# q transposed on VectorE in 32x32 blocks, kv and u on eight TensorE tiles, one PSUM ring and a new hand-written order

## The chip, the cores and the metric

The kernel runs on one core of a Trainium2 chip. The metric is device time in microseconds (us) of one execution; the time before is the median of three runs. The engines are named as the profile names them: PE is TensorE (its matmuls; PEld its weight loads), DVE is VectorE, ACT is ScalarE, POOL is GpSimd, SP is SyncE, which here only issues DMAs.

## What is computed

A linear attention with a normalised output, followed by a channel mix. B = 8 batches, H = 8 heads, S = 576 positions, 64 dims per head; all inputs and the output are fp32. C = 512, F = 1024.

```python
def _attn_ref(q, k, v, g_norm):
    kv = np.einsum('bhsd,bhse->bhde', k, v)
    out = np.einsum('bhsd,bhde->bhse', q, kv)
    rms = np.sqrt(np.mean(out * out, axis=-1, keepdims=True) + 1e-06)
    return (out / rms * g_norm).astype(np.float32)

def _moe_ref(x, mu_k, mu_r, w_k, w_v, w_r):
    x_prev = np.concatenate([np.zeros((B, 1, D)), x[:, :-1, :]], axis=1)
    xk = mu_k * x + (1.0 - mu_k) * x_prev
    xr = mu_r * x + (1.0 - mu_r) * x_prev
    k = np.maximum(xk @ w_k, 0.0)
    v = k * k @ w_v
    r = 1.0 / (1.0 + np.exp(-(xr @ w_r)))
    return (r * v).astype(np.float32)
```

The attention's heads are laid side by side as the 512 channels of x. Matmuls run in bf16 with fp32 sums in PSUM.

## The kernel before, in words

**Layout.** All activations of the second half stand with channels on the partitions: a batch's x is four chunks of 128 channels (two heads each, e = 0 and 1), handled as two halves z = 0 and 1 of two chunks each (y). k, v and q are loaded by POOL DMAs that cast to bf16, with position s = 9p + j on 64 partitions p per head and nine column blocks j (NJ = 9, NP = 64). The kernel keeps that permuted order of positions (j, then p) up to the stores.

**Attention of one batch** (`attention`, line 362). `kv` (L286): for each head nine matmuls of 64x64 sum k.T v; four heads' tiles are in use at a time. `q` (L294): 36 transposes of 64x64 per half through the identity matrix into PSUM, then a copy `qc` to SBUF on ACT or DVE. `u` (L301): kv times q, per half z and half of the positions i, four matmuls of 64x64 tiles over 288 columns. `uc` copies u to bf16, `sq` squares it (ACT from PSUM, or DVE from the copy), `ss` sums the squares over a head's 64 dims by a matmul (with a block of 1/64 for batches 0 and 1, L432 and L464; with 32 columns per chunk, L409, and a spread by eight SP DMAs per batch, `sp`, L455, from batch 2 on). `rs` (L306) is the reciprocal root on ACT, `mul` (L423) the product of u and rs into an x buffer `xT`.

**The blend** (`blends`, line 311). In the permuted order the position before is 64 columns earlier, and the first block's predecessors are the last block's, shifted by one: `wr` copies those 63 columns in front of `xT`. Then `d` = cur - prev (L318), `mk` and `mr` = d times mu (a scalar per partition, L178 on ACT or L180 on DVE), `xk` and `xr` = m + prev (L331), written to a ring of four batches. In batch 0 this is done in parts `a`, `b` and a wrapped part `w`.

**The channel mix** (`mix`, line 496) works on nine groups g of 512 positions. `k` (L542; L518 for group 0): eight blocks of four matmuls, `relu` on ACT, `ksq` on DVE; `r` (L564): four blocks of four, `sig` on ACT; `v` (L584): four rows of 128 positions in two parts of four matmuls, `out` on DVE = v times sig, `st` the stores on SP (row blocks of up to 64 positions, so mostly two DMAs each). g_norm is put into w_k and w_r in place (`g.wk`, `g.wr`), by a column `cols` that a small matmul `tr9` makes from mu_k, mu_r and g.

**The order.** Each piece of work has a name such as `u3.01` or `k4.6`, registered by `add` with what it depends on. The text `ORDER` lists the names; `emit` (line 84) issues them in that order, so it is each engine's own order, with `@A` (ACT) or `@D` (DVE) where a choice is open. `ld.*` are the load DMAs on POOL. `z:512` is a matmul of zeros on PE that nothing needs. PSUM is four tiles of two banks, two of them tagged `mm` (for k, r, v) and two `at` (for the attention and `ss`); SBUF buffers are rings too (k, v, q three each, qT, uT four or three).

Of the kernel before, what the change touches and what calls it, by code (L numbers as in the profile page):

```python
# [7 lines left out]
FP32 = mybir.dt.float32  # L8
BF16 = mybir.dt.bfloat16
# [6 lines left out]
ld.q0.0 seta small setb ld.k0.0 ld.v0.0 ld.q0.1 ld.v0.1 ld.k0.1 ident ld.wk0 id9 ld.q1.0 z:512 z:512 z:512 z:512  # L16
z:512 z:512 z:512 z:512 z:512 z:512 z:512 q0.01 ld.wk1 tr9 qc0.01@A cols z:512 q0.00 qc0.00@A ld.v1.1 z:512 z:512
z:512 z:512 z:512 z:512 z:512 z:512 kv0.0 ld.v1.0 kc0.0@A z:512 u0.01 u0.00 uc0.01@D uc0.00@A ld.k1.1 sq0.01@D
sq0.00@D z:512 z:512 z:512 z:512 z:512 ss0.01 ss0.00 rs0.01 ld.k1.0 rs0.00 mul0.01 z:512 z:512 q0.11 qc0.11@D ld.wr
mul0.00 z:512 kv0.1 q0.10 d0.0a kc0.1@A qc0.10@D mk0.0a@A z:512 u0.11 uc0.11@D u0.10 wr0.0@A sq0.10@A d0.0w sq0.11@D  # L20
uc0.10@A g.wk00@D ld.q1.1 z:512 z:512 z:512 z:512 ss0.10 xk0.0a d0.0b ss0.11 rs0.10 k0.000 ld.wv0 rs0.11 mul0.10
q1.0 g.wk01@A d0.1a mk0.1a@D mk0.0b@A xk0.1a mr0.0a@D table k0.001 g.wk10@D ld.wv1 g.wk11@D k0.010 mul0.11 relu0.00
d0.1b ld.q2.01 xk0.0b k0.011 mk0.0w@D mk0.1b@D k0.100 wr0.1@D relu0.01 xk0.1b ld.v2.01 d0.1w ksq0.00 k0.101 mr0.0b@A
mr0.1a@D k0.110 ld.k2.01 relu0.10 xr0.0b ksq0.01 mr0.1b@A xk0.0w ksq0.10 ld.v3.01 kv1 qc1.0@D kc1@A xr0.1b mr0.0w@A
xr0.0a u1.01 u1.00 uc1.01@A k0.111 uc1.00@A g.wr1@D ld.k3.01 g.wr0@D relu0.11 sq1.01@D r0.2 sq1.00@D ld.q3.01
mr0.1w@D mk0.1w@D ss1.0 xr0.0w ss1.1 ksq0.11 rs1.0 r0.3 xr0.1a rs1.1 q1.1 r0.0 qc1.1@D ld.k6.01 xr0.1w mul1.0 u1.11
sig0.1 u1.10 r0.1 uc1.11@D sq1.10@A v0.1.0 sq1.11@D sig0.0 xk0.1w ld.q4.01 uc1.10@D ss1.2 v0.1.1 wr1.0@D d1.0 ss1.3
v0.0.0 mk1.0@D rs1.2 xk1.0 v0.0.1 ld.v4.01 rs1.3 q2.0 mul1.1 q2.1 qc2.0@A v0.3.0 wr1.1@D d1.1 v0.3.1 out0.0 mk1.1@A
v0.2.0 st0.1 qc2.1@A xk1.1 v0.2.1 mr1.1@D k1.2 out0.1 k1.3 mr1.0@D kv2 relu1.1 k1.0 kc2@D ld.k4.01 xr1.0 ld.q5.01
u2.10 u2.01 uc2.10@D k1.1 uc2.01@A sq2.01@A sq2.10@D k1.6 relu1.0 u2.11 u2.00 uc2.11@A k1.7 uc2.00@D sq2.11@D k1.4  # L30
sq2.00@A xr1.1 relu1.3 k1.5 ksq1.3 ss2 kv3 ksq1.1 rs2 q3.0 ld.k5.01 sp2.0 r1.0 kc3@A relu1.2 qc3.0@D r1.1 ksq1.0
u3.01 q3.1 uc3.01@D sp2.1 r1.2 ld.q6.01 sq3.01@D ld.v5.01 r1.3 sig1.0 qc3.1@D ld.v6.01 ksq1.2 u3.00 u3.10 v1.0.0
uc3.00@D uc3.10@A st0.0 sq3.10@A sq3.00@D v1.0.1 sig1.1 mul2.0 u3.11 q4.1 wr2.0@D d2.0 v1.1.0 mk2.0@A v1.1.1 mul2.1
v1.3.0 qc4.1@A out1.0 v1.2.0 wr2.1@A xk2.0 uc3.11@A st1.0 v1.2.1 sq3.11@A d2.1 v1.3.1 st0.3 mk2.1@D xk2.1 ss3 kv4
out1.1 q4.0 k2.2 ld.q7.01 qc4.0@D rs3 ld.v7.01 k2.3 kc4@D sp3.0 mr2.1@D u4.11 u4.00 uc4.11@D k2.4 uc4.00@A relu2.1
sq4.11@D k2.5 sq4.00@D sp3.1 mr2.0@D u4.01 relu2.2 u4.10 uc4.01@D k2.0 sq4.10@A sq4.01@D k2.1 ksq2.1 uc4.10@A st1.1
xr2.0 ss4 relu2.0 q5.1 xr2.1 k2.6 ksq2.0 k2.7 mul3.0 qc5.1@D r2.0 relu2.3 r2.1 wr3.0@A ksq2.3 rs4 r2.2 ksq2.2 sp4.0
d3.0 r2.3 sig2.0 mk3.0@D q6.1 mul3.1 kv5 sig2.1 q5.0 qc6.1@D st1.3 v2.3.0 kc5@A qc5.0@D v2.1.0 st0.2 wr3.1@D d3.1
u5.11 u5.01 sp4.1 uc5.11@A v2.2.0 mk3.1@D uc5.01@A xk3.1 v2.3.1 mr3.1@D v2.2.1 sq5.01@D st1.2 sq5.11@D v2.0.0 xk3.0
out2.1 u5.10 kv6 uc5.10@A q6.0 ld.k7.01 mul4.0 v2.0.1 st2.2 qc6.0@A mr3.0@D v2.1.1 kc6@A sq5.10@D st2.3 xr3.1 k3.2  # L40
out2.0 u6.10 u5.00 k3.3 uc5.00@A mul4.1 st2.0 k3.4 xr3.0 relu3.1 wr4.1@D k3.5 d4.1 uc6.10@A r3.0 mr4.1@D relu3.2
sq5.00@D r3.1 sq6.10@D wr4.0@D ksq3.1 u6.01 sig3.0 ss5 uc6.01@D k3.0 d4.0 k3.1 sq6.01@D mk4.1@D rs5 kv7 mr4.0@D
relu3.0 q7.0 sp5.1 xr4.0 u6.00 k3.6 kc7@A ksq3.2 qc7.0@A k3.7 mk4.0@D ksq3.0 r3.2 relu3.3 sp5.0 uc6.00@D r3.3
sq6.00@D xk4.0 u6.11 q7.1 uc6.11@D v3.1.0 st2.1 ksq3.3 v3.0.0 sig3.1 mul5.1 v3.1.1 qc7.1@A sq6.11@D xk4.1 ss6 xr4.1
v3.0.1 r4.0 out3.0 r4.1 rs6 st3.0 u7.10 u7.11 sq7.10@A v3.2.0 uc7.11@A st3.1 uc7.10@D v3.3.0 sq7.11@D wr5.1@D sp6.0
u7.00 mul5.0 u7.01 v3.2.1 sig4.0 d5.1 v3.3.1 uc7.00@A wr5.0@A k4.6 sq7.00@A out3.1 sq7.01@A k4.7 uc7.01@A mk5.1@D
st3.2 ss7 d5.0 relu4.3 k4.2 sp6.1 mk5.0@D mr5.1@A k4.3 xk5.0 k4.4 ksq4.3 relu4.1 xr5.1 k4.5 xk5.1 k4.0 relu4.2
mul6.0 k4.1 mr5.0@D wr6.0@A d6.0 r4.2 relu4.0 r4.3 ksq4.0 k5.2 ksq4.1 sig4.1 mul6.1 k5.3 ksq4.2 v4.1.0 mr6.0@D rs7
xr5.0 v4.1.1 relu5.1 sp7.1 v4.0.0 wr6.1@A ksq5.1 v4.0.1 r5.0 out4.0 sp7.0 r5.1 mk6.0@D v4.3.0 d6.1 v4.2.0 mr6.1@D
st4.1 sig5.0 mk6.1@D v4.3.1 xk6.0 v4.2.1 k5.4 out4.1 k5.5 xr6.0 st4.3 k5.0 relu5.2 xk6.1 k5.1 mul7.1 st4.0 wr7.1@A  # L50
k5.6 relu5.0 d7.1 st3.3 k5.7 ksq5.0 k6.6 ksq5.2 relu5.3 xr6.1 k6.7 mk7.1@D k6.0 relu6.3 mr7.1@D k6.1 ksq6.3 r6.2
# [48 lines left out]
def kernel(  # L100
# [20 lines left out]
    NJ = 9  # L121
    NP = S // NJ
    HS = S // 2
    NZ = NHP // 2
# [6 lines left out]
    CB = 2  # L131

# [8 lines left out]
        "q": (3, (128, NHP, NJ * HD), BF16),  # L141
        "kv": (2, (128, 2, NZ * HD), BF16),
        "qT": (4, (128, 2, S), BF16),
# [10 lines left out]
        "mm": (2, (128, 2, 512), FP32),  # L154
        "at": (2, (128, 2, 512), FP32),
# [4 lines left out]
    def get(buf, dtype=None):  # L160
        if buf.t is None:
            n, shape, dt = BUFS[buf.tag]
            pool = psum if buf.tag in ("mm", "at") else sb
            buf.t = pool.tile(list(shape), dt, tag=buf.tag, name=buf.tag, bufs=n)
        return buf.t

    def as_bf16(ps):
        return get(ps)[:, :, :].bitcast(BF16)
# [21 lines left out]
    ident = const.tile([128, 128], BF16, name="ident")  # L190
# [12 lines left out]
    xTs = [const.tile([128, 2, NP + S], BF16, name=f"xT{i}") for i in range(NX)]  # L203

    src = {"k": k, "v": v, "q": q}
    kvq = {(n, b): Buf(n) for n in src for b in range(B)}

    def setup_a(_):
        nc.vector.memset(zero, 0.0)  # L209
        nc.vector.memset(ident, 0.0)  # L210

    def setup_b(_):
        nc.vector.memset(eps, 1e-6)
        nc.vector.memset(ones, 0.0)
# [12 lines left out]
    def small_loads(_):
# [134 lines left out]
    def attention(b):  # L362
# [28 lines left out]
        else:  # L391
# [261 lines left out]
```

## Time and profile before

| what | value |
|---|---|
| median of three runs | 209.66 us (209.08 to 210.3) |
| span of the profiled execution | 206.6 us |
| granted TensorE clock, mean | 1.000 |
| PE: transposes of q (L294) | 576 matmuls, 8.0 us busy |
| PE: kv (L286) and u (L301) | 576 and 128 matmuls, 6.4 and 7.9 us busy |
| PE: k, r, v (L518, L542, L564, L584) | 7.6 + 59.2 + 34.1 + 66.6 us busy |
| ACT relu, sig, table loads | 36.8, 18.3, 15.4 + 1.3 us busy |
| loads: q, k, v and weights | 35 DMAs on POOL, 16.78 MB as written |
| HBM read, written | 33.56 MB, 9.44 MB |

The profile is of one execution, and its span, 206.6 us, runs from its first instruction to its last; the median of the runs is 3.06 us longer, and that difference is taken as what lies around the span. Matmuls are pipelined, so a duration of one, such as 379 ns, is longer than the distance to the next, 0.216 us for 512 columns (16 of them in 3.45 us on the chain of waits). Lines with PE in them are known by L294 (transposes of q), L286 (kv), L301 (u), L409, L432 and L464 (sums of squares), L482 (zeros), and L518, L542, L564, L584 (k, r, v).

### The profile page before, as it was taken

The numbers are of one execution on the slowest core, as the hardware profiler recorded it, in microseconds if no ns is written. First come the engines' busy times: TensorE is split into PE (matmuls) and PEld (weight loads), VectorE is DVE, ScalarE is ACT, GpSimd is POOL, SyncE is SP. The second block draws the span as 40 slices with busy tenths as digits, with TensorE's granted clock in tenths as the row PEclk, the third lists the DMA queues.
The fourth block names the chain that finished last, engine by engine and source line by source line (L and its number), as shares of the span: only waits on it lengthen the run. The fifth ranks groups of instructions, "written<-read, shape, count | busy, mean of one in ns | idle before, by whom it ended". The sixth has DMA issues, their size and how long they took to land.

```text
span 206.6 us, 5133 instructions
## 1 busy us (share of the span) xinstructions
PE 193.2 (94%) x2172; PEld 95.7 (46%) x2172; DVE 137.8 (67%) x273; ACT 118.6 (57%) x151; POOL 26.4 (13%) x40
## 2 busy tenths in 40 slices
PE   7797979999799799799999999999999999999992
PEld 2344844544344444354443585444444444444441
DVE  1059988886585999698997798788733623421332
ACT  2279789867577395636896987716725032531310
POOL 7752532202140400000000000000000000000000
PEclk9999999999999999999999999999999999999999
DMA  4999999999999999999433650346004242604155
GB/s 75 162 207 205 206 208 205 208 216 221 210 238 236 231 252 242 223 264 268 116 91 77 149 122 0 71 94 156 0 0 102 62 93 61 143 0 102 24 133 153
DMA packets 25211, 30.10 MB, mean 146 GB/s; under 512 B 2524, under 2 KB 20708, under 8 KB 25188
## 3 DMA queue, kind: packets, MB, share of 16 engines
q0 software_dynamic: 15408, 16.78, 48.3%
q1 hardware_dynamic: 9380, 12.46, 24.0%
q10 hardware_dynamic: 400, 0.52, 0.7%
q8 instruction: 17, 0.28, 0.5%
q14 instruction: 6, 0.05, 0.1%
HBM read 33.56 MB, written 9.44 MB: 208 GB/s over the span
## 4 chain that ended last, share of the span: by engine, by line
PE 68%; DMA 20%; SPq 3%; ACT 2%; POOL 2%; issue 2%; DVE 1%; ACTq 0%; DVEq 0%; POOLq 0%
PE mm L584 26%; PE mm L542 24%; PE mm L564 12%; DMA w_r<-in_moe_w_r_dram 7%; DMA rs<-rsc 5%; DMA k<-in_k_dram 4%; DMA out_dram<-out 3%; SPq L455 2%; PE at L584 2%; PE at L301 2%; PE at L286 1%; PE at L294 1%; SPq L493 1%; POOL q L251 1%; ACT rsc L306 1%
## 5 line engine op out<-in xcount | busy, mean ns | idle before, releaser
L584 PE MATMUL mm<-w_v,sqk 128*128 128x512 bf16 x272 | 62.6, 379 | 0.0
L542 PE MATMUL mm<-xk,w_k 128*128 128x512 bf16 (+1 forms) x288 | 59.2, 356 | 0.0
L503 ACT ACTIVATE relu<-mm 128x1024 bf16<-128x1024 f32 x36 | 36.8, 1022 | 25.8 <-PE mm L542 23.4
L584 PEld LDWEIGHTS <-sqk 128*128 128x128 bf16 x296 | 28.2, 98 | 32.2 <-issue 1.4
L542 PEld LDWEIGHTS <-w_k 128*128 128x128 bf16 x288 | 27.2, 98 | 26.9 <-issue 1.6
L564 PE MATMUL mm<-w_r,xr 128*128 128x512 bf16 x144 | 34.1, 379 | 0.7 <-DVE w_r L180 0.7
L552 DVE TENSOR_TENSOR sqk<-relu 128x1024 bf16<-128x1024 bf16 x32 | 21.6, 687 | 16.4 <-ACT relu L503 16.4
L597 DVE TENSOR_TENSOR out<-mm,sig 128x1024 f32<-128x1024 f32 x16 | 19.6, 1222 | 18.6 <-PE mm L584 18.6
L574 ACT ACTIVATE sig<-mm 128x1024 bf16<-128x1024 f32 x18 | 18.3, 1024 | 22.5 <-PE mm L564 22.5
L564 PEld LDWEIGHTS <-xr 128*128 128x128 bf16 x144 | 13.7, 98 | 16.6 <-issue 1.0
L180 DVE TENSOR_SCALAR md<-d,cols 128x576 bf16<-128x576 bf16 (+2 forms) x62 | 18.2, 344 | 0.3
L172 ACT CAST uT<-at 128x576 bf16<-128x576 f32 (+1 forms) x18 | 11.4, 645 | 11.4 <-PE at L301 11.3
L423 DVE TENSOR_TENSOR xT<-uT,rs 128x1152 bf16<-128x1152 bf16 (+2 forms) x18 | 12.4, 686 | 4.8 <-DMA rs<-rsc 3.0
L188 ACT ACT_TABLE_LOAD x12 | 15.4, 1283 | 0.2
L174 DVE CAST uT<-at 128x576 bf16<-128x576 f32 (+1 forms) x14 | 10.4, 742 | 7.0 <-PE at L301 5.5
L318 DVE TENSOR_TENSOR d<-xT 128x1152 bf16<-128x1152 bf16 (+2 forms) x20 | 12.7, 634 | 0.8 <-ACT xT L172 0.5
L331 DVE TENSOR_TENSOR xk<-md,xT 128x1152 bf16<-128x1152 bf16 (+2 forms) x20 | 12.7, 633 | 0.6 <-ACT md L178 0.4
L331 DVE TENSOR_TENSOR xr<-md,xT 128x1152 bf16<-128x1152 bf16 (+2 forms) x20 | 12.5, 631 | 0.0
L482 PE MATMUL mm<-zero 128*128 128x512 bf16 x34 | 10.9, 452 | 1.2 <-DVE zero L209 1.2
L172 ACT COPY qT<-at 128x1152 bf16<-128x1152 bf16 (+2 forms) x8 | 8.0, 995 | 6.0 <-PE at L294 6.0
L178 ACT ACTIVATE md<-d,cols 128x256 bf16<-128x256 bf16 (+2 forms) x18 | 9.9, 600 | 1.8 <-DVE d L318 1.8
L174 DVE COPY qT<-at 128x1152 bf16<-128x1152 bf16 (+2 forms) x10 | 6.9, 693 | 4.7 <-ACT kv L172 4.2
(54 smaller groups left out, 139.3 us busy)
## 6 DMA issues: line engine op xcount, KB each, us to landing
out_dram<-out SPq DMA_DIRECT2D x67, 128.0 KB, 2.5
q<-in_q_dram POOLq DMA_DIRECT2D x6, 576.0 KB, 23.0
v<-in_v_dram POOLq DMA_DIRECT2D x6, 576.0 KB, 25.7
k<-in_k_dram POOLq DMA_DIRECT2D x6, 576.0 KB, 22.5
rs<-rsc SPq DMA_DIRECT2D x48, 72.0 KB, 5.0
q<-in_q_dram POOLq DMA_DIRECT2D x4, 288.0 KB, 9.7
k<-in_k_dram POOLq DMA_DIRECT2D x4, 288.0 KB, 11.4
v<-in_v_dram POOLq DMA_DIRECT2D x4, 288.0 KB, 11.0
```

What stands on the lines that cost most here:

```text
L172: nc.scalar.copy(out=dst, in_=src)
L174: nc.vector.tensor_copy(out=dst, in_=src)
L180: nc.vector.tensor_scalar(out=dst, in0=src, scalar1=col, scalar2=None, op0=ALU.mult)
L188: nc.scalar.preload_act_table_set(name)
L331: nc.vector.tensor_tensor(out=dst[:, 2 * z:2 * z + 2, r0:r0 + w], in0=md.t[:, :, cs], in1=xT[:, :, prev], op=ALU.add)
L503: nc.scalar.activation(out=get(rt), in_=ps.t, func=AF.Relu)
L542: nc.tensor.matmul(get(ps)[:, fc % 2, a0:a1], w_k_sb[:, cc, 128 * fc:128 * fc + 128], xk[:, cc, x0:x0 + a1 - a0], start=(cc == 0), stop=(c ...
L552: nc.vector.tensor_mul(out=get(sqk)[:, 2 * f2:2 * f2 + 2, :], in0=rt.t, in1=rt.t)
L564: nc.tensor.matmul(get(ps)[:, ci % 2, :], xr[:, cc, n0:n0 + 128], w_r_sb[:, cc, :], start=(cc == 0), stop=(cc == NHP - 1))
L574: nc.scalar.activation(out=get(sg), in_=ps.t, func=AF.Sigmoid)
L584: nc.tensor.matmul(get(ps)[:, bank, cs], sqk.t[:, fc, 128 * ci:128 * ci + 128], w_v_sb[:, fc, cs], start=(fc == 0), stop=(fc == NFC - 1))
L597: dv = add(f"out{g}.{c2}", "D", lambda _, ps=ps, sg=sg, ot=ot: nc.vector.tensor_mul(out=get(ot), in0=ps.t, in1=sg.t), deps=ms + [sg_done], ...
```

## The change

- **q.** The load takes q as it lies in memory: partition p holds 36 consecutive positions of one head (16 partitions per head), 2304 bf16 values. Read as fp32, a value is a pair of dims. DVE transposes blocks of 32x32 of these pairs (`tq`, two instructions per batch, 18 blocks each), writing with a step of 36 fp32 elements, so that positions come out in natural order. Chunk m's pairs of dims then stand on partitions 32m to 32m + 31, and head e's positions in columns S*e on, the two dims of a pair (r) next to each other. The PE transposes, their copies `qc` and the 128x128 identity go; a 9x9 one stays for `tr9`.
- **kv and u.** kv takes every second column of k for each r and writes 32 partitions per chunk: 144 matmuls of 64x32 tiles per batch, eight tiles in turn. u sums r = 0 and 1: 16 matmuls of 32x64 tiles per word, each over 288 columns, reading every second element of qT. A word `u3.01.0` covers both halves z (batch 0 has one word per z), and so two PSUM tiles.
- **g** is the factor of the u copy `uc` (ACT or DVE); the weights are used as loaded. `sq` reads u, without g, from PSUM, and only on ACT.
- **Natural order.** `wr` and batch 0's `w` parts go; prev is the column just before cur. `xk` = cur + (mu - 1) * d, so `cols` gets mu - 1. A store is one DMA of 128 rows.
- **PSUM** is one ring of four tiles, `ps`, for everything; the zero matmuls hold one of them until group 0.
- **Loads**: w_k in halves of rows instead of columns; the order after batch 0 is wk0, wk1, wr, batch 1, wv0, wv1, batch 2.
- **Order**: all words in a new order. Choices of engine: `uc` 14 on ACT and 18 on DVE (were 18 and 14), `mk` and `mr` 15 and 21 (9 and 31), `kc` 5 and 4 (7 and 2); `sq` 32 on ACT (10 on ACT, 22 on DVE). Table loads of ACT between rs and sig by the order: 9 (were 11).

```diff
@@ ORDER, its head @@
-ld.q0.0 seta small setb ld.k0.0 ld.v0.0 ld.q0.1 ld.v0.1 ld.k0.1 ident ld.wk0 id9 ld.q1.0 z:512 z:512 z:512 z:512
...
+seta ld.q0.0 ld.k0.0 ld.v0.0 tq0.0.1 setb tq0.0.0 ident ld.q0.1 ld.v0.1 ld.k0.1 small
+zz z:512 z:512 z:512 z:512 z:512 z:512 z:512 z:512 z:512 z:512 tr9 z:512 z:512 z:512 z:512 z:512 z:512 z:512 z:512 z:512 z:512 z:512 z:512 z:512 z:512 z:512 z:512 z:512 z:512 z:512 z:512 z:512 z:512 z:512 z:512 kv0.0 cols ld.wk0 ld.wk1 kc0.0@D z:512 u0.0.0 uc0.00@D ld.wr u0.0.1 uc0.01@D
+tq0.1.0 ld.v1.0 tq0.1.1 ld.q1.01 ld.k1.1 sq0.00 z:512 ss0.00 sq0.01 ld.k1.0 ld.v1.1 ss0.01 z:512 z:512 z:512 kv0.1
+ld.wv0 rs0.01 mul0.01 rs0.00 kc0.1@A z:512 z:512 z:512 u0.1.0 u0.1.1 ld.wv1 sq0.10 z:512 ss0.10 mul0.00 d0.01
+mk0.01@D d0.00 mr0.01@D uc0.10@A mk0.00@D rs0.10 mul0.10 ld.v2.01 sq0.11 z:512 z:512 z:512 z:512 z:512 ss0.11 xk0.01 k0.100
+ld.k2.01 d0.10 mk0.10@D xk0.00 uc0.11@A rs0.11 mul0.11 k0.000 k0.010 k0.110 d0.11 xk0.10
+mk0.11@A xk0.11 xr0.01 mr0.11@D k0.011 mr0.10@A xr0.10 mr0.00@A xr0.00 k0.101 relu0.01 xr0.11
+k0.111 relu0.10 relu0.11 ksq0.10 r0.2 r0.3 sig0.1 r0.0 ld.q2.01 k0.001 relu0.00 r0.1
+tq1.01.0 ksq0.11 ksq0.01 kv1.01 tq1.01.1 kc1.01@D u1.01.0 ksq0.00 sig0.0 table sq1.10 u1.01.1
+sq1.11 sq1.00 sq1.01 uc1.10@D v0.2.0 uc1.11@D ss1.2 v0.3.0 uc1.01@D uc1.00@D rs1.2 ss1.3
+rs1.3 mul1.1 ss1.1 rs1.1 ss1.0 rs1.0 d1.1 mul1.0 mk1.1@A d1.0 mr1.1@D v0.3.1
+xk1.1 mk1.0@A v0.1.0 v0.1.1 v0.0.0 v0.2.1 mr1.0@A v0.0.1 xk1.0 out0.0 kv2.01 kc2.01@A
+k1.0 k1.1 relu1.0 out0.1 st0.3 k1.2 tq2.01.1 k1.3 relu1.1 tq2.01.0 u2.01.0 sq2.10
...
@@ buffers @@
-        "q": (3, (128, NHP, NJ * HD), BF16),
-        "kv": (2, (128, 2, NZ * HD), BF16),
-        "qT": (4, (128, 2, S), BF16),
+        "q": (3, (128, QJ * HD), BF16),
+        "kv": (2, (128, 2, 2 * HD), BF16),
+        "qT": (2, (128, 2 * S, 2), BF16),
...
-        "mm": (2, (128, 2, 512), FP32),
-        "at": (2, (128, 2, 512), FP32),
+        "ps": (4, (128, 2, 512), FP32),
@@ kv, u @@
+    def kv_tiles(ps, kin, vin, ms):
+        for r in range(2):
+            for j in range(NJ):
+                for m in ms:
+                    for e in range(2):
+                        rows_ = slice(64 * e, 64 * e + 64)
+                        nc.tensor.matmul(ps[32 * m:32 * m + 32, e, HD * r:HD * r + HD],
+                                         kin[rows_, m, HD * j + r:HD * j + HD:2], vin[rows_, m, HD * j:HD * j + HD],
+                                         start=(j == 0), stop=(j == NJ - 1))
+
+    def u_tiles(pss, kv, qT, zs, c0, c1):
+        for r in range(2):
+            for z in zs:
+                for y in range(2):
+                    for e in range(2):
+                        m = 2 * z + y
+                        rows_ = slice(32 * m, 32 * m + 32)
+                        nc.tensor.matmul(pss[z][64 * e:64 * e + 64, y, 0:c1 - c0], kv[rows_, e, HD * r:HD * r + HD],
+                                         qT[rows_, S * e + c0:S * e + c1, r], start=(r == 0), stop=(r == 1))
@@ blends @@
-        cur, prev = slice(NP + x0, NP + x0 + w), slice(x0, x0 + w)
+        cur, prev = slice(X0 + x0, X0 + x0 + w), slice(X0 - 1 + x0, X0 - 1 + x0 + w)
...
-in0=md.t[:, :, cs], in1=xT[:, :, prev],
+in0=md.t[:, :, cs], in1=xT[:, :, cur],
@@ attention @@
+                def tq(_, i=i, part=part):
+                    src = qin.t.bitcast(FP32).rearrange("q (j i) -> q j i", i=32)
+                    dst = get(qT).rearrange("q t r -> q (t r)").bitcast(FP32).rearrange("q (p j) -> q j p", j=QJ)
+                    js = slice(QJ // 2 * i, QJ // 2 * i + QJ // 2)
+                    nc.vector.transpose(out=dst[part, js, :], in_=src[part, js, :])
...
+                uc = add("uc" + name, "DA", lambda eng, ps=ps, uT=uT, cs=cs, w=w: scale(
+                    eng, get(uT)[:, :, cs], ps.t[:, :, 0:w], cols[:, 8:9]), deps=[pu[(z, i)], p_cols], bufs=[ps, uT])
+                sq_ = add("sq" + name, "A", lambda _, ps=ps, sq=sq, cs=cs, w=w: nc.scalar.activation(
+                    out=get(sq)[:, :, cs], in_=ps.t[:, :, 0:w], func=AF.Square), deps=[pu[(z, i)]], bufs=[ps, sq])
@@ store @@
+    def store(g, ci, ot, cs=slice(None), eng=None):
+        row = G * g + 128 * ci
+        (eng or nc.sync).dma_start(out=out_rows[row:row + 128, cs], in_=ot)
```

QP = 16, QJ = 36 and X0 = 2 are new constants.

## The prediction

> **What bounds it now.** I read the page first, then the chain of waits in order of time, then the timeline of PE, ACT, DVE and POOL in the first 45 us and of PE between 45 and 104 us, last the groups split by shape.
>
> ```profile
> span 206.6 us, 5133 instructions
> PE 193.2 (94%) x2172; PEld 95.7 (46%) x2172; DVE 137.8 (67%) x273; ACT 118.6 (57%) x151; POOL 26.4 (13%) x40
> ...
> PE   7797979999799799799999999999999999999992
> ...
> DVE  1059988886585999698997798788733623421332
> ...
> DMA  4999999999999999999433650346004242604155
> ```
> PE is full from about 30 us to 203 us; the 16 DMA engines are full until about 95 us; VectorE (DVE) is near full in several slices between 60 and 115 us, but seldom the last to arrive. The chain in order of time (start, length, what):
>
> ```profile
> 29.04 0.89 DVE w_r L180 x2
> ...
> 29.97 1.02 PE mm L564 x4
> ...
> 43.43 1.73 PE mm L542 x8
> 45.16 0.74 PE at L286 x72
> 45.89 0.97 PE mm L542 x4
> 46.86 0.37 PE at L301 x8
> ...
> 91.00 0.25 PE at L301 x4
> ...
> 201.05 1.76 PE at L584 x16
> ```
> So before 30 us the loads decide (w_r lands at 29.0), and after it the work of PE itself. PE's own idle after 30 us is small, and the timeline names it:
>
> ```profile
> 54.39 0.48 PE L294 MATMUL at<-ident,q 64*64 64x64 bf16 x36 [1.20 <-DMA q<-in_q_dram]
> ...
> 68.42 0.83 PE L286 MATMUL at<-v,k 64*64 64x64 bf16 x72 [0.93 <-DMA k<-in_k_dram]
> ...
> 71.81 0.44 PE L301 MATMUL at<-qT,kv 64*64 64x288 bf16 x8 [0.42 <-DVE kv L174]
> ...
> 84.16 0.77 PE L286 MATMUL at<-v,k 64*64 64x64 bf16 x72 [1.42 <-ACT sig L574]
> ```
> Together 4.0 us. I cut the span at the first k matmul of group 1: 43.4 us to it, 159.4 us from there to PE's end at 202.8, 3.8 us of last product and store. The runs shown have a median of 209.66, so 3.06 us lie around the span.
>
> **Stage 1, up to group 1.** A hand chain in the new order, with these rows: a load of 288 KB lands every 1.45 us and one of 512 KB every 2.6 (POOL's timeline, where each issue waits for the load eight before it; all landings here are counted on from k0.1 at 14.4); 512 columns of PE 0.216 us; u copies 0.64 to 0.75, squares 0.65, rs 0.74 and 1.28 per table load on ACT; mul, d and x 0.42 to 0.48 at batch 0. Thirty-five zero matmuls now stand ahead of kv0.0, with tr9 among them: 4.56 us for the first eleven as in the trace, 24 more at 0.215, so kv0.0 starts at 11.1 (was 9.95). The copy kc0.1 now waits on ACT behind rs0.01, rs0.00 and their table load until 16.0 (was 15.3); behind it stand u0.1 and all of heads 4 to 7. First k matmul 19.7 (was 18.4). But w_r comes third among the weights, at 22.1 instead of 29.0, so k0 and r0 (7.0 + 3.5 us) run through to 30.8, the time at which v1.1, now last of batch 1, lands too. kv1, u1 follow to 32.4. v0 then needs a PSUM tile of the four that u1 holds: freed when ACT, after sig0.0 and a table load, has squared one, 34.1; PE idles 1.3 us. The rest of v0 and kv2 (k2 lands at 41.7) fill PE while batch 1 goes through rs, mul, d, md, xk; xk1.0 is done at 42.75. **Group 1 starts at 42.8 instead of 43.4: -0.6**, and kv2 is already behind it: **-0.7**. Bounds: 41 (no PSUM wait) to 45 (a late v1.1 and k2).
>
> **Stage 2, PE's own work.** The transposes go: ten words q3.0 to q7.1 of 36 stood on this stretch, 0.30 to 0.55 us each by the starts that follow them, **-4.05**. kv doubles from 72 to 144 matmuls per batch. Now the 72 start within 0.57 us, 8 ns a pair, plus 0.17 of fill, 0.74. If eight tiles overlap twice as well as four, 144 cost the same 0.74; if a pair keeps 8 ns, 1.32. No row has this; the eight L301 weight loads, of four tiles, follow one another every 5.7 ns (0.14 us in all, 0.10 for one), the nearest start rate, which gives 1.0: **+0.3 x 5 = +1.5** for kv3 to kv7 (0 to +2.9). u: four matmuls on four tiles cost 0.25, eight 0.37, so 0.12 per round. A word is now 16 on eight tiles, two rounds, 0.37; twelve words 4.4 against 4.5 in the trace now: **0** (up to 0.61 a word, +2.9, if only four run together). The moving rows step over every second element; I take no price, the +2.9 covers it. ss is unchanged.
>
> **Stage 2, the other engines.** None adds to the sum while PE covers it, so I check the load. Off DVE: qc 6.9, sq 9.6, g 2.6, wr 1.5, ten md pieces about 6, batch 0's wrapped d and x 1.2. On DVE: 18 block transposes of 576 fp32 elements. Lower bound the cast of as many fp32 elements, 0.75; upper the product of 1024 fp32 elements, 1.22. I take 0.75, 13.5 in all, as the count of elements is the same; plus four more u copies, 3.0. DVE falls by some 11 us. ACT loses qc 8.0, wr 2.3, g 1.1, four u copies 2.6, two table loads 2.6, small md pieces 1.5, and gains 22 squares of 0.65, 14.4, and eight md pieces of 1.43, 11.4: +8. The words from group 1 to kv7, at these means, sum to 44 us on each. DVE's groups overlap (its words now sum to 151.5 against 137.8 busy, 0.91; ACT's to 122.4 against 118.6, 0.97), so 40 us of DVE and 43 of ACT stand beside 49 of PE: 82% and 87%. The same sums now give DVE 88% and ACT 70% of PE and its idle over the stretch from group 1 to r3. If that cover failed, a late xk would hold k of the next group, and late squares u's tiles.
>
> g in the u copy costs nothing: the copy is there already, and its factor lands with tr9, 5 us before. `d` reads `prev` one bf16 element off:
>
> ```profile
> L318 DVE TENSOR_TENSOR d<-xT 128x1152 bf16<-128x1152 bf16 x14 | 10.6, 754 | 0.5 <-ACT xT L172 0.4
> ...
> L174 DVE COPY xT<-xT 128x126 bf16<-128x126 bf16 x8 | 1.5, 191 | 0.1
> ```
> The second row starts its output on an odd element, and its 126 elements cost only some 25 ns above the 169 of a nine-element copy: it ran at the fast rate. So d stays 0.754 (up to about 1.36, the fp32 product's rate, 8 us of DVE). [...]
>
> Loads: the same bytes. q is one run of 9 KB per partition instead of four of 2.3 KB; priced at zero. In the new order k3 lands near 50.4 and q3 near 53.3, where PE wants them at about 50.5 and 54, so the waits for loads stay about as now. On SP the 74 store issues become 37 of 0.6 us, so rs spreads queue behind fewer; on POOL the order is changed, not the number by more than one, and q7 holds v7, v6, k6, k7 until tq4 is done near 66, while q5 and v5 are in flight until about 73. One PSUM ring: a u word takes two of four tiles, so relu, sig and squares on ACT free what k, r and v wait for. I keep PE's idle at the present **4.0** (0 to 8). Tail: same last quarter, copy and store, **0**.
>
> Sum: 206.6 - 0.6 - 0.7 - 4.05 + 1.5 = 202.75, plus 3.06 around it: **205.8; I say 205.5**, giving 0.3 to better overlap of kv.
>
> **Rivals.**
> (a) The waits vanish: loads in the order of use, half the store issues, less DVE. For it: 2.1 of the 4.0 us wait for loads, k6 now goes ahead of k4. Against: DMA is full to 95 us either way and kv7 wants the last load at about 95. 205.5 - 4 = **201.5**.
> (b) Slower: the block transpose writes with a step of 36 fp32 elements (144 bytes), and if that takes a second cycle per element (0.60 us for 576), one costs 1.36. From group 1 to kv7 twelve of them then add 7 us to DVE's 40: 47 beside PE's 49, and held to the 88% that DVE reaches now, 54. It decides from about 1.1 us each on, when 40 + 12 x 0.35 passes 88% of 49 and idle; at 1.36 it is +5 for that stretch and 1 for the six of the head: **211.5**. For it: no row has such a step. [...]
> [...]
> (c) The tiles don't run eight at a time: kv 1.32, u 0.61: 205.5 + 1.4 + 2.9 = **209.8**, so nearly the whole gain is gone.
> (d) ACT is the new bound: a u word ends with two squares (1.3 us) behind a relu (1.0) before its tiles are free, against 0.9 to 1.7 us of k that cover it; 0.4 us lost at each of twelve words, +5: **210.5**. For it: the 1.42 behind sig above. Against: DVE at 88% costs PE 0.42 us now.
>
> **Chances.** Forecast 0.42, (a) 0.20, (b) 0.14, (c) 0.08, (d) 0.16. A measurement of this kernel can't tell less than 0.5%, 1.05 us, from no change: faster is under 208.6, which is all of (a) and nearly all of the forecast, 0.59; (c) and the upper edge of the forecast give 0.11 for the same; (b) and (d) 0.30. The range runs from under (a) to over (b), 200 to 213; the forecast's own is 203 to 208.
>
> **What would show it.** No L294 left and PE's k of group 1 near 43 us; L301-like bursts of 16 in about 0.4 us and 144 kv in about 1.0; DVE transposes at 0.75 us, d at 0.75; PE idle after 43 us near 4. Wrong if transposes take over 1.3 us with PE waiting for DVE, if u bursts take 0.6, or if PE waits for ACT's squares.

## The result and the profile after

The changed kernel takes **232.08 us** (median of 4 runs, 230.36 to 233.26) against 209.56 us of the kernel before (four runs): a ratio of 1.105, 95% interval 1.098 to 1.112. The forecast was 205.5 us; the time lies far outside the range of 200 to 213 and is no rival's.

The page of the changed kernel: span, busy time, then PE's busy tenths and the granted TensorE clock (PEclk) in 40 slices of 5.7 us.

```profile
span 228.4 us, 5332 instructions
PE 204.4 (90%) x2315; PEld 98.7 (43%) x2315; DVE 137.2 (60%) x226; ACT 125.5 (55%) x160; POOL 23.6 (10%) x39
...
PE   7978993998798789999766999999999999999993
...
PEclk9999997699979979999995999999999999999999
```

The transposes on PE are gone, and yet PE is busy 11 us longer than before (193.2). The row PEclk says why in part: in slices 6, 7, 11, 14 and 21 (counted from 0) the granted clock is 0.5 to 0.7; in the profile before, it was 1.00 throughout. The slices with little PE work, 3 at slice 6 and 6 at 20 and 21, lie among or beside them. The chain of waits (start, length, what) shows the places where PE stops:

```profile
33.03 1.34 PE ps L292 x144
...
34.87 0.56 PE ps L303 x17
35.44 3.43 issue
38.87 0.70 PE ps L303 x12
...
49.77 1.28 PE ps L292 x144
51.05 3.57 PE ps L511 x16
...
60.27 1.05 PE ps L292 x116
61.32 1.98 issue
63.30 0.30 PE ps L292 x28
...
78.52 2.02 issue
...
116.36 2.18 issue
...
120.30 1.97 issue
```

L292 is kv, L303 is u, and 51.05 is the first k matmul of group 1, forecast for 42.8. "issue" is idle time in which PE waited for nothing that the profile shows. At 61.32 it stops within kv3, behind 116 of its 144 matmuls: nothing inside a row of such matmuls can be waited for, since they read two tiles that are there and write one that is theirs. There are five such stops: 3.43 us at 35.4, 1.98 at 61.3, 2.02 at 78.5, 2.18 at 116.4, 1.97 at 120.3, **11.6 us** together. The clock falls during the first, and within 1.2 us behind each of the next three; the fifth lies in the spell of the fourth. The windows at the first (length, busy time by engine, then clock, DMA share and GB/s):

```profile
35.00:37.00 2.00, 0.44 (x17) 0.13 (x9) 1.23 (x2) 1.10 (x2) 0.90 (x2) 1.00 1.22 212
37.00:39.00 2.00, 0.13 (x8) 0.13 (x15) 0.00 (x0) 0.00 (x0) 0.24 (x1) 0.55 1.21 206
39.00:41.00 2.00, 2.00 (x19) 0.64 (x17) 0.68 (x1) 1.36 (x3) 0.00 (x0) 0.50 1.19 221
```

PE runs again from 38.9, but at half clock until 44. Half-clock spells lie at 37.0 to 44.0, 64.5 to 68.0, 81.5 to 85.0 and 119.0 to 126.0, so each lasts 3.5 or 7 us. PE's busy time in half-us windows, times what the clock lacked, sums to **8.4 us**.

**Why does PE stop there?** I counted the matmuls that PE had run at each stop: 476, 859, 1114, 1625 and 1753. The differences, 383, 255, 511 and 128, are 3, 2, 4 and 1 times 128 to within one. A matmul here comes with a weight load, so 128 of them are 256 instructions. The DMA queue that the page calls "instruction" moved 0.29 MB in 18 packets, 16 KB each; the 2315 matmuls and their weight loads make 18.1 blocks of 256.

```profile
q8 instruction: 18, 0.29, 0.5%
```

So theory **F**: PE's program arrives in blocks of 256 instructions; a block takes some 3.5 us or more to arrive; a row of 144 tiny matmuls eats one in 1.3 us, so PE stops at the end of a block, and the idle time halves the clock. From the start of a block to the resumption I estimated 5.5 us at the first stop and 3.3 to 3.7 at the others. Counted 128 matmuls back from each stop, it is 5.5, 4.7, 3.5, 3.4 and 3.7 us; the first two stops lie where the DMA engines are full (share 1.2), the other three where they are all but idle (0.02). The rival, R: the stops come from what happens at these places (contention, a wait that the trace hides), and what costs is the rest of the change, its transposes of 1.20 us, its copies and squares of u and its order.

### The profile page after: what moved, and what is told of

Its sections match the earlier page's. It is cut to its first block, busy times and chain, and to the rows that moved or that the text cites. A ratio compares the mean times of both kernels' runs of the same rounds, so it can differ in the third digit from the quotient of the medians.

```text
span 228.4 us, 5332 instructions
## 1 busy us (share of the span) xinstructions
PE 204.4 (90%) x2315; PEld 98.7 (43%) x2315; DVE 137.2 (60%) x226; ACT 125.5 (55%) x160; POOL 23.6 (10%) x39
## 4 chain that ended last, share of the span: by engine, by line
PE 77%; DVE 7%; issue 7%; ACT 4%; DMA 3%; SPq 0%; ACTq 0%; DVEq 0%
PE ps L553 25%; PE ps L511 21%; PE ps L533 14%; PE ps L455 4%; PE ps L292 4%; DMA out_dram<-out 3%; PE ps L487 3%; DVE uT L188 2%; PE ps L303 2%; ACT sq L388 1%; ACT L196 1%; DVE out L566 1%; PE ps L397 1%; ACT relu L470 1%; DVE md L188 1%
## 5 line engine op out<-in xcount | busy, mean ns | idle before, releaser
L553 PE MATMUL ps<-w_v,sqk 128*128 128x512 bf16 (+1 forms) x296 | 69.2, 384 | 1.0 <-DVE sqk L521 0.8
L511 PE MATMUL ps<-xk,w_k 128*128 128x512 bf16 (+1 forms) x288 | 59.8, 359 | 0.5 <-ACT sq L388 0.3
L470 ACT ACTIVATE relu<-ps 128x1024 bf16<-128x1024 f32 x36 | 36.4, 1022 | 28.3 <-PE ps L511 28.0
L566 DVE TENSOR_TENSOR out<-ps,sig 128x1024 f32<-128x1024 f32 x16 | 19.4, 1220 | 30.5 <-PE ps L553 10.4
L533 PE MATMUL ps<-w_r,xr 128*128 128x512 bf16 x144 | 36.7, 404 | 0.2 <-ACT sq L388 0.2
L388 ACT ACTIVATE sq<-ps 128x576 bf16<-128x576 f32 (+2 forms) x32 | 19.9, 650 | 27.2 <-DVE uT L188 18.4
L543 ACT ACTIVATE sig<-ps 128x1024 bf16<-128x1024 f32 x18 | 18.2, 1022 | 19.4 <-PE ps L533 19.3
L188 DVE TENSOR_SCALAR uT<-ps,cols 128x576 bf16<-128x576 f32 (+2 forms) x18 | 14.1, 813 | 18.1 <-PE ps L303 10.8
L367 DVE STREAM_TRANSPOSE qT<-q 128x576 f32<-128x576 f32 (+1 forms) x18 | 20.8, 1195 | 3.9 <-DMA q<-in_q_dram 3.9
L186 ACT ACTIVATE md<-d,cols 128x576 bf16<-128x576 bf16 (+2 forms) x30 | 19.6, 714 | 2.3 <-DVE d L320 2.3
L303 PE MATMUL ps<-qT,kv 32*64 32x288 bf16 (+2 forms) x256 | 9.5, 313 | 9.2 <-issue 5.4
L455 PE MATMUL ps<-zero 128*128 128x512 bf16 x49 | 14.3, 436 | 1.2 <-DVE ident L216 1.2
L292 PE MATMUL ps<-v,k 64*32 64x64 bf16 x1152 | 11.1, 197 | 4.2 <-issue 4.2
L292 PEld LDWEIGHTS <-k 64*32 64x32 bf16 x1152 | 9.8, 90 | 7.6 <-issue 7.3
## 6 DMA issues: line engine op xcount, KB each, us to landing
k<-in_k_dram POOLq DMA_DIRECT2D x6, 576.0 KB, 18.4
```

The lines of the kernel that those rows point to most:

```text
L188: nc.vector.tensor_scalar(out=dst, in0=src, scalar1=col, scalar2=None, op0=ALU.mult)
L292: nc.tensor.matmul(ps[32 * m:32 * m + 32, e, HD * r:HD * r + HD], kin[rows_, m, HD * j + r:HD * j + HD:2], vin[rows_, m, HD * j:HD * j + H ...
L367: nc.vector.transpose(out=dst[part, js, :], in_=src[part, js, :])
L388: sq_ = add("sq" + name, "A", lambda _, ps=ps, sq=sq, cs=cs, w=w: nc.scalar.activation(out=get(sq)[:, :, cs], in_=ps.t[:, :, 0:w], func=AF ...
L455: nc.tensor.matmul(get(k_ps[(0, 0)])[:, 0, 0:n], zero[:, 0:128], zero[:, 0:n], start=not started, stop=not started)
L470: nc.scalar.activation(out=get(rt), in_=ps.t, func=AF.Relu)
```

## The experiments

Ratios are against the kernel before, run beside each group (209.78 to 210.13 us). e1, e4 and e6 leave blocks of k or q in other places than the result needs, so only their time is used.

| run | what | us | ratio, 95% interval |
|---|---|---|---|
| e1 | change, kv of batches 1 to 7 by 72 matmuls | 218.94 | 1.0422 [1.0367, 1.0477] |
| e2 | change, each kv in four pieces between other words | 220.25 | 1.0502 [1.0454, 1.0551] |
| e3 | before, kv by 144 matmuls | 225.62 | 1.0762 [1.0717, 1.0806] |
| e4 | change, transposes write densely | 230.2 | 1.0975 [1.0921, 1.1029] |
| e5 | e2, squares read the SBUF copy | 218.81 | 1.0456 [1.0403, 1.0508] |
| e6 | e2, transposes write densely | 219.18 | 1.0463 [1.0423, 1.0503] |
| e7 | e2, 8 zero matmuls fewer | 221.03 | 1.0555 [1.0499, 1.0611] |
| e8 | change, 8 zero matmuls fewer | 227.6 | 1.0866 [1.0804, 1.0928] |
| e10 | e6 with u reading in natural order | 224.09 | 1.0686 [1.0628, 1.0744] |
| e11 | e5, e7 and e10 together | 223.72 | 1.0646 [1.0581, 1.071] |
| e12 | e3 with kv in pieces | 220.2 | 1.0496 [1.045, 1.0541] |
| e13 | before, 1008 kv matmuls at its end | 237.24 | one run beside 210.13 |

**e1: half as many matmuls.**

```diff
+    def kv_tiles72(ps, kin, vin):
...
+                        nc.tensor.matmul(ps[64 * y:64 * y + 64, e, HD * z:HD * z + HD], kin[rs_, 2 * z + y, cs],
+                                         vin[rs_, 2 * z + y, cs], start=(j == 0), stop=(j == NJ - 1))
...
-            m = add("kv" + name, "T", lambda _, ps=ps, zs=zs: kv_tiles(get(ps), kin.t, vin.t, range(2 * zs[0], 2 * zs[-1] + 2)),
+            m = add("kv" + name, "T", lambda _, ps=ps, zs=zs: kv_tiles72(get(ps), kin.t, vin.t) if b else kv_tiles(
```

> The changed kernel with kv of batches 1 to 7 made by 72 matmuls of 64x64 tiles, as before the change, into the same PSUM columns (the sums stand in other places, so u multiplies other numbers); everything else, the order included, is as changed. Theory F (instruction supply: PE stops at every 256th instruction when the 256 before it were used up in less time than the next block takes to arrive, 3.3 to 5.5 us, and the stop of 2 us or more halves its clock for some us): the bursts shrink from 144 + 16 matmuls to 72 + 16, less than a block, so most of the 11.6 us of stops and most of the 7.3 us lost to the half clock go, with 7 x 0.55 us of kv: 232 falls to 208 to 214. Rival R (the loss comes from the new order, from squares only on ACT and from PSUM): only kv's 4 us go, 226 to 229.

218.94 us: 13 of the 22.5 us are gone, so the time lies between the two answers, 5 above F's and 7 below R's; F has the larger part, and something else is left. One stop is left, 2.19 us, behind kv6 and kv7, which stand in a row and are again 144 matmuls. Those took 1.35 us as 64x64 tiles, against 1.28 for 144 of 64x32: the time goes by the matmul, hardly by the size of its tile. Part of what is left shows in the trace, which is of the longest run (221.66 us): PE waits 5.49 us for xk in one place, and half clock costs 6.6 us.

**e2: the same 144, but not in a row.**

```diff
-    def kv_tiles(ps, kin, vin, ms):
-        for r in range(2):
-            for j in range(NJ):
+    def kv_tiles(ps, kin, vin, ms, rj=None):
+        for r, js in rj or [(r, range(NJ)) for r in range(2)]:
+            for j in js:
...
-v1.2.0 v1.0.1 kv4.01 uc3.00@A ss3 rs3 sp3.1 v1.3.1 mk2.1@D xk2.1 mr2.0@A ld.k5.01 v1.2.1 out1.1 st1.3 k2.6 ld.q4.01 kc4.01@A
+v1.2.0 v1.0.1 kv4.01a uc3.00@A ss3 rs3 sp3.1 v1.3.1 kv4.01b mk2.1@D xk2.1 mr2.0@A ld.k5.01 v1.2.1 kv4.01c out1.1 st1.3 k2.6 kv4.01d ld.q4.01 kc4.01@A
```

> The changed kernel with each kv of batches 1 to 7 cut into four pieces of 40, 32, 40 and 32 matmuls, with one k, r or v word of four matmuls between the pieces; the number of instructions is the same. Theory F: 128 matmuls now take 3 us or more almost everywhere, so most stops and half-clock stretches go though not one instruction less is issued: 212 to 219. Rival R: no change, 229 to 234. A third theory, that a PSUM tile held longer or a later kv costs PE more than it gains, would show as waits for ACT or DVE and a time above 232.

220.25 us, 1.25 above F's bound. The longest stop is 0.62 us; one half-clock spell is left, 37.0 to 44.0. So the same number of instructions, with the same work, costs 11.8 us less when nothing but their places differ (those of kv, and of four copies kc that follow it). Idle times of 0.16 to 0.22 us, which the trace shows at some ten of the joins, are no price of cutting: a matmul's record is missing there. The trace holds 2315 weight loads and 2283 matmuls; at such a join, at 33.5 us, it has the four weight loads of a word of r and three of its four matmuls.

**e3: give the kernel before the same row.**

```diff
-                        nc.tensor.matmul(ps[64 * y:64 * y + 64, e, c + HD * z:c + HD * z + HD], kin[rs_, 2 * z + y, cs],
-                                         vin[rs_, 2 * z + y, cs], start=(j == 0), stop=(j == NJ - 1))
+                        for h in range(2):
+                            o, kc_ = 64 * y + 32 * h, HD * j + 32 * h
+                            nc.tensor.matmul(ps[o:o + 32, e, c + HD * z:c + HD * z + HD], kin[rs_, 2 * z + y, kc_:kc_ + 32],
+                                             vin[rs_, 2 * z + y, cs], start=(j == 0), stop=(j == NJ - 1))
```

> The kernel before with each kv matmul cut into two of 64x32 tiles, 144 per batch, same result, same order. Theory F: kv costs 0.55 us more per batch (4.4) and where kv stands next to 36 transposes, 180 matmuls in a row, a whole block fits in the burst in some of the eight cases: stops of about 2 us with a half clock behind them, 5 to 12 us; 217 to 226. Rival R: only the 4.4, 213 to 215.

225.62 us, at F's upper end, 10 above R's. There are stops of 0.63, 0.76, 3.54, 2.40 and 4.36 us, and 4.7 us are lost at half clock. The three long ones:

```profile
52.23 0.40 PE L303 MATMUL at<-qT,kv 64*64 64x288 bf16 x5 [3.54 <-issue]
...
65.87 0.31 PE L296 MATMUL at<-ident,q 64*64 64x64 bf16 x13 [2.40 <-issue]
...
83.81 0.69 PE L296 MATMUL at<-ident,q 64*64 64x64 bf16 x34 [4.36 <-issue]
```

26 records of matmuls are missing here, so I count by the weight loads, which are all there: the stops stand behind 222, 476, 860, 1115 and 1371 of them, at differences of 254, 384, 255 and 256. The changed kernel stops behind 476, 859, 1115, 1625 and 1753: at 476, 859 or 860 and 1115 two programs with different work stop at the same count. In this kernel a row of kv goes on with a row of transposes, so two of the stops lie within those. The order, the transposes on VectorE and the copies of u are not needed for the stops.

**e4: the transposes' step.**

```diff
-                    dst = get(qT).rearrange("q t r -> q (t r)").bitcast(FP32).rearrange("q (p j) -> q j p", j=QJ)
+                    dst = get(qT).rearrange("q t r -> q (t r)").bitcast(FP32).rearrange("q (j p) -> q j p", j=QJ)
```

> The changed kernel with the block transposes writing each 32x32 block next to the last instead of with a step of 36 fp32 elements (the positions of q come out block by block, so u's columns belong to other positions). If the step costs the 0.44 us by which a transpose is over 0.75, they fall from 1.20 to about 0.75. Theory F: PE doesn't wait for them, the time stays within 1%, 230 to 233. My second rival of the prediction (late transposes hold PE): 224 to 228.

A transpose falls to 761 ns from 1196, so the step of 144 bytes in its output costs 0.44 us each; the time is 230.2, 1.9 less, with intervals that overlap.

**e5, e6, e7: what is left of e2.** e2's span is 219.4 us, 12.8 over the kernel before: 3.8 up to the first k matmul (22.2 instead of 18.4), 2.4 from there to group 1 (half clock, 2.7), 6.6 behind it, of which 5.7 are more idle time of PE in the trace (some 1.3 of it stand where records are missing). I tried one suspect each: the copy and the square of one PSUM tile, the transposes, and the zero matmuls that stand ahead of kv0.0. The edits (e6 has e4's; e7 takes 8 of the 24 zero matmuls between tr9 and kv0.0 out of the order):

```diff
@@ e5 @@
-                    out=get(sq)[:, :, cs], in_=ps.t[:, :, 0:w], func=AF.Square), deps=[pu[(z, i)]], bufs=[ps, sq])
+                    out=get(sq)[:, :, cs], in_=uT.t[:, :, cs] if b else ps.t[:, :, 0:w], func=AF.Square,
+                    scale=cols[:, 9:10] if b else 1.0), deps=[uc if b else pu[(z, i)]], bufs=[uT if b else ps, sq])
```

> e2 (220.25 us) with the squares of batches 1 to 7 reading the SBUF copy of u with factor 1/g instead of the PSUM tile; same words, where a copy stood behind its square it now stands just ahead of it. In e2, 6.6 us of PE's own waits after 30 us name a copy or square of u, a transpose or a square-based word (uT 1.38 and 0.90, sq 1.30 and 0.3, sqk 0.83, out 0.82, rsc 0.84). Theory S (copy and square of one PSUM tile run one after the other, and the tile is held for both, 1.4 to 1.55 us): a tile is free after the copy alone, 0.75 to 0.81 us, and the waits that name uT and sq fall from 3.9 to about 1: 216.5 to 218.5 us. Rival: the square still waits for the copy, and other words are ready no sooner, so the waits only change their names: 219.5 to 221.5 us.

> e2 (220.25 us) with the transposes writing blocks next to each other (q's positions stand elsewhere in qT, so u is that of permuted positions), 0.76 us instead of 1.20. With the instruction stops gone they could now set the pace: theory T (the transposes are a good part of what is left above the kernel before): at least 2 us less, 216 to 218.3. Rival: only the waits that name qT fall (1.57 us on one u word), and DVE has room elsewhere: 218.3 to 220.5 us, about 0.5 to 1.9 less.

> e2 (220.25 us) with 8 of the 34 zero matmuls ahead of kv0.0 left out (1.7 us of PE at full clock). kv0.0 starts at 11.80 there and at 9.95 in the kernel before; the first k matmul at 22.22 (18.4 before). Theory H (the zeros hold kv0.0, and from it one chain of copy, square, rs, product, d, md, xk sets the first k matmul): kv0.0 at about 10.1, first k matmul at 20.5 to 20.9, time 1.3 to 1.8 us less, 218.4 to 219. Rival: loads of w_k or DVE's other work set the first k matmul, at 22: no change, 219.8 to 220.7 us.

e5: 218.81 us, 0.3 above theory S's bound. The waits that name copies and squares are shorter, and group 1 starts at 46.4 instead of 49.6, but a stop of 2.69 us has come up in kv3's first piece of 40. So S is borne out in its direction; its size is mixed with the stop. e6: 219.18, the rival's answer, 1.1 less; a difference of this size is at the edge of what the intervals of e2, e5 and e6 tell apart. e7: the chain of theory H holds (first k matmul at 20.5), and group 1 starts 2.6 us sooner, but the time does not follow: PE now waits 1.23 us for v's load ahead of kv1, and one stop of 1.30 us is back in kv3. At 221.03 (220.14 to 222.19) it is no faster than e2: what the head gains is lost again behind it.

**e8: move the work by eight matmuls against the blocks.** The edit is e7's, on the changed kernel.

> The changed kernel (232.08 us) with the same 8 zero matmuls left out and nothing else. Theory F (PE's instructions come in blocks of 128 matmuls and their weight loads, counted from the program's start): the first stop of over 1.5 us comes again when about 476 matmuls have run, so 8 matmuls later in the work: behind 25 of the 32 u matmuls that follow kv1, and the second behind 124 of kv3's 144 (859); differences between stops again multiples of 128. Time 229.5 to 232.5. Rival (a stop belongs to the place in the burst, or to what waits there): the stops stay at 17 u matmuls behind kv1 and 116 of kv3, at 468 and 851 matmuls run.

The timeline of PE in e8 (start, length, line, shape, count, and idle time ahead with its cause); in the changed kernel the u row broke into 17 and 15, here:

```profile
32.84 0.69 PE L298 MATMUL ps<-qT,kv 32*64 32x288 bf16 x25 [0.56 <-DVE kv L177]
36.84 0.46 PE L298 MATMUL ps<-qT,kv 32*64 32x288 bf16 x7 [3.32 <-issue]
...
64.02 0.35 PE L287 MATMUL ps<-v,k 64*32 64x64 bf16 x20 [4.49 <-issue]
```

25 and 7; and the stop in kv3 came with 20 of its matmuls left instead of 28, the one in kv7 with 106 instead of 114. By the weight loads the stops stand behind 476, 859, 1625 and 1753 again, as F said: they stay with the count from the program's start, eight matmuls later in the work. The time, 227.6, fell by 4.5 us where F allowed 2.6 at most, though one stop grew to 4.49. Where a boundary falls in the work changes what it costs: the one at 1115 stood behind a row and cost 2.02 us, and now has long v matmuls ahead of it and costs 0.32.

**e10, e11: can the step be moved to PE, and do the parts add?**

```diff
-                                         qT[rows_, S * e + c0:S * e + c1, r], start=(r == 0), stop=(r == 1))
+                                         qT[rows_, S * e + c0:S * e + c1, r] if not dense else qT.rearrange(
+                                             "q (j p) r -> q p j r", p=32)[rows_, QP * e + c0 // QJ:QP * e + c1 // QJ, :, r],
+                                         start=(r == 0), stop=(r == 1))
```

> e2 (220.25 us) with the transposes of batches 1 to 7 writing their blocks next to each other, as in e6 (219.18), and u's matmuls reading qT with a step of 64 bf16 elements per row instead of 2, so that positions come out in natural order. Account A (PE reads moving rows at any step alike): transposes 0.76 us, u bursts of 16 in 0.39 to 0.45 as now, 218.5 to 220 us. Rival (the longer step slows PE's reading): bursts of 0.5 us and more, twelve of them from group 1 on, 220.5 to 223 us.

> e2 (220.25 us) with all three parts at once: squares from the copy (e5, -1.4), dense transposes read with a step (e6, -1.1), 8 zero matmuls fewer (e7, +0.8 with overlapping runs, so taken as 0). If the parts are waits at different places they add: 216.8 to 218.2 us. Rival (they hide the same waits): 218.2 to 219.5 us. Neither comes near the kernel before, 209.8: a version below 213 would mean that the accounts of e2 (head +3.8, up to group 1 +2.4, PE's work +0.9, PE's idle +5.7) miss something.

e10 takes 224.09 us, the rival's side and 1.1 over its bound: a u matmul takes 650 ns instead of 297 in e2, and a row of 16 takes 1.15 us instead of 0.46.

```profile
L300 PE MATMUL ps<-qT,kv 32*64 32x288 bf16 x224 | 7.3, 297 | 4.8 <-DVE qT L368 1.6 <-DVE uT L185 0.9 <-DVE kv L179 0.9
...
L300 PE MATMUL ps<-qT,kv 32*64 32x288 bf16 x224 | 17.0, 650 | 1.7 <-DVE kv L179 0.9 <-DVE qT L371 0.8
```

The first line is e2's, the second e10's.

e11 contains this loss, so its 223.72 (both answers missed) says nothing on whether the other parts add.

**e12: the row of e3, cut.** The four pieces a to d of a batch's kv, as in e2, in the kernel before with 144:

```diff
-kv3 ksq1.1 rs2 q3.0 ld.k5.01 sp2.0 r1.0 kc3@A
+kv3a kv3b ksq1.1 rs2 r1.0 kv3c kv3d q3.0 ld.k5.01 sp2.0 kc3@A
```

> The kernel before with 144 kv matmuls per batch (e3, 225.62 us), each batch's in four pieces of 40/32/40/32 with k, r or v words between (kv1 and kv3 partly). Theory F: without stops only the pairs' own time is left, 0.54 to 0.7 us for each of seven batches, 4 to 5 us: 213 to 216 us, no stop above 1 us, granted clock 1.00. Rival (the 144 matmuls cost as such, by contention or by the PSUM tile that they hold): 219 us and more.

220.2 us: the cut is worth 5.4 us, but F's figure was missed by 4, and the time is the rival's. The trace has another reason than the rival gave: stops of 0.68, 1.84 and 1.20 us are left behind batch 0, now at u and within the 36 transposes that follow the last pieces, and one half-clock spell lost 1.6 us. Without these it would be 215, inside F's range, but that is a subtraction and was not run. The rows were made shorter, not short enough.

**e13: the supply by itself.**

```diff
+    ps_b, k7, v7 = Buf("at"), kvq[("k", 7)], kvq[("v", 7)]
+    add("burst", "T", lambda _: [kv_tiles(get(ps_b), 0, k7.t, v7.t, range(NZ)) for i in range(14)], bufs=[ps_b, k7, v7])
```

> The kernel before with 1008 more kv matmuls of 64x64 tiles (batch 7's k and v, fourteen times its 72, into a PSUM tile that nobody reads) in one row behind the last product: nothing waits for them, nothing else runs beside them but the last stores. Theory F (a block of 128 matmuls and weight loads takes 3.3 to 3.7 us to be supplied, whatever the DMA load, from the starts of a block to the resumption in the changed kernel): PE runs 128 to 256 matmuls at 8 ns, stops, and then goes on at one block per 3.3 to 3.7 us, stops at differences of 128; the row takes 20 to 28 us, 224 to 235 us in all. Rival (the stops come from what the kernel does around them): 1008 at 8 ns, 8.1 us, no stop over 1 us, 213 to 215 us.

```profile
204.34 2.92 PE L295 MATMUL at<-v,k 64*64 64x64 bf16 x221
208.97 1.24 PE L295 MATMUL at<-v,k 64*64 64x64 bf16 x128 [1.72 <-issue]
212.70 1.93 PE L295 MATMUL at<-v,k 64*64 64x64 bf16 x128 [2.49 <-issue]
216.70 1.92 PE L295 MATMUL at<-v,k 64*64 64x64 bf16 x128 [2.08 <-issue]
220.43 1.92 PE L295 MATMUL at<-v,k 64*64 64x64 bf16 x128 [1.80 <-issue]
```

This settles that the supply stops PE. PE runs 221 matmuls, and then exactly 128 at a time, one block per **3.73 to 4.00 us** (the starts), with the DMA engines all but idle (share 0.02). At full clock a block lasts 1.24 us, 9.7 ns a matmul; from the second stop on the clock is 0.50 to the end, and it lasts 1.92. The instruction queue moved seven packets more than in the kernel before (24 against 17). The row took 28.3 us, 0.3 over F's upper end; a block is some 0.3 us dearer than I had estimated, and the total, 237.24, is 2 above the bound. The rival's 213 to 215 is out. It was run once, and it says nothing on "whatever the DMA load": where the DMA engines were full, a block took 4.7 to 6.2 us by the same count (changed kernel, e3, e8), though no run varied the DMA load alone.

In rows of tiny matmuls, then, the wait for the next block stands open: 1.97 to 3.43 us each time in the changed kernel and up to 4.49 in e8.

No version tried comes under the kernel before; the fastest, e5, is 4.6% slower, with kv's cuts and one stop still in it.

## Why the prediction was wrong

The span is 25.65 us above the sum of 202.75: 8.25 in stage 1 (51.05 instead of 42.8), 17.4 from group 1 to PE's end, 0 in the tail.

- **The step that failed is the price of kv's 144 matmuls**: +1.5 us, bounds 0 to +2.9, as time of PE alone. The row of 8 ns a pair was there, but I priced what one pair costs and never asked what feeds 144 of them in a row. The stops cost 11.6 us (3.4 of them in stage 1) and the half clock behind them up to 8.4 (2.6 in stage 1), 20 of the 25.65 us. e2 and e8 show that it is the row and its place against the blocks, e3 that it is not the rest of the change, e13 that it is supply. With the 1.4 and the 2.5 us of the next two points, 1.7 us stay unnamed.
- **The same term, its size**: 1.28 us per batch on the chain instead of 1.0, close to 1.32, the upper of my two bounds, +1.4 for five batches. The weight loads of four tiles at 5.7 ns were the wrong nearest row.
- **Stage 1's head** was 2.5 us late (first k matmul at 22.2, not 19.7). kv0.0 started 0.7 later than I counted (11.8), and the squares stood behind the copies: at batch 0 the first two copies of u take 1.54 us from 13.58 on, and the first square starts at 14.36, when the first copy is done, on another engine and without needing it. I had let both start when u was there.
- **The copy and the square of u**, therefore, hold a PSUM tile for both, 1.4 us, and not for one. Rival (d) named squares as the holder, for 5 us; PE's waits that name a copy or square of u behind group 1 are 1.3 us in the changed kernel, and e5 took 1.4 from e2.
- **The transposes** cost 1.196 us, not 0.75, close to the upper bound of 1.22; the step in the output is the cause, as rival (b) said (e4). That rival's 6 us did not come: written densely, they are worth 1.9 us with the stops (e4) and 1.1 without (e6), each barely told from nothing. No run shows the cycle that it counts with; its 0.60 us is an estimate, 1.04 ns an element, the rate at which the fp32 products on VectorE grow in the kernel before (424, 692 and 1222 ns for 256, 512 and 1024 elements). Measured, the step costs 0.44.
- **Missed and small**: with g as a factor a copy of u takes 813 ns on VectorE and 740 on ACT, 60 and 100 more than a plain one (752 and 640 before). I had it at nothing.

Right were: u in 0.39 to 0.41 us a row, so eight tiles do run at once there (rival (c) falls for u; its 1.32 for kv came close); the tail, 3.8; and `d` with its odd offset. PE's idle time behind group 1 without the stops came out at 4.2 us for 4.0, but that was luck: none of it waits for a load, as 2.1 us did before, and 1.6 wait for a product `out` on VectorE, 0.8 each for a copy of u and a `ksq`. The lines of `d` and of the transpose:

```profile
L320 DVE TENSOR_TENSOR d<-xT 128x1152 bf16<-128x1152 bf16 x14 | 10.6, 755 | 0.8 <-ACT md L186 0.6
...
L367 DVE STREAM_TRANSPOSE qT<-q 128x576 f32<-128x576 f32 x14 | 16.1, 1196 | 0.0
```

755 ns against the 754 of before: the odd offset of `prev` cost nothing, and the 1.36 us that I had allowed as the upper bound did not come.

**What stays open.** During or behind every "issue" stop of 1.97 us or more in these traces the clock halves, and so it does behind some waits for another engine (5.49 us for xk in e1, 2.36 for sig in e13). What PE idle time starts it is not settled: a wait of 2.01 us in e1 and the stop of 1.72 in e13 did not, a spell at 37 us in e2 follows pauses of 0.66 and 0.62 us, and spells from 14.5 us on in e5 and from 16.0 on in e4 and e6 follow pauses of at most 0.88. The kernel before was granted a mean clock of 0.99 in many of its runs beside the experiments. So the 8.4 us are what half clock cost, not all of them shown to come from the stops. Of the nine us that e5 has over the kernel before, a stop and waits on several engines are named, but none was measured alone.

## What to carry to other kernels

Count instructions, not only time: at 128 matmuls (with their weight loads) per 3.7 to 4 us, measured with the DMA engines all but idle (e13), PE can be fed a matmul about every 30 ns over a longer stretch, and a row of some 150 shorter ones can end in a stop and half clock. Whether it does depends on where the blocks end. In the changed kernel kv1, kv3 and kv4 met a stop, and their blocks had been used up in 1.5 to 2.7 us; kv2 and kv5 are the same rows and ran through, as a block ended within each and the next lasted 8.2 and 5.4 us. Where a change splits matmuls into smaller tiles, put the pieces between long matmuls (worth 11.8 us in e2, 5.4 in e12), and look for "issue" idle time in the middle of a row, at multiples of the same count. A saving on one engine is worth its own length only if what replaces it is as cheap to supply as to execute: here 11.6 us of stops came with it.

## What the hardware did that I had not expected

- The stops: 221 matmuls, then 128 per 3.73 to 4.00 us, with almost nothing else running (e13); in the changed kernel, e3 and e8 at the same counts of weight loads (476 and 859 or 860 in all three), whatever the work.
- Half-clock spells of 3.5 or 7 us, and a clock that stays at 0.50 while blocks of 1.92 us alternate with pauses of 1.8 to 2.1 (e13).
- The time of tiny matmuls goes by their number, 9 to 10 ns each in rows, with 64x64 as with 64x32 tiles (1.35 and 1.28 us for 144; e1, the changed kernel).
- Reading moving rows at a step of 64 bf16 elements takes a matmul of 288 columns 650 ns, against 297 at a step of 2 (e10, e2).
- VectorE's block transpose takes 761 ns with dense output and 1196 with a step of 144 bytes (e4).
- A copy and a square that only read the same PSUM tile ran one after the other on their two engines. In the changed kernel the first two copies of u start at 13.58 us and end by 15.12; the squares start at 14.36 and 15.15, each as its copy ends. What orders them is not shown.
